# Query products in two cuts, x partly normalised by GpSimd, key normalisation shared in more ways, and a new order

## The chip, the cores and the metric

The kernel runs on one core of a Trainium2 chip. The core has five engines that run their own queues of instructions and wait for one another through semaphores: TensorE (PE in the profile; its weight loads are PEld), VectorE (DVE), ScalarE (ACT), GpSimd (POOL) and SyncE (SP), which here only starts DMA transfers. The metric is the device time of one execution in microseconds (us); lower is better. The time before is the median of three runs.

## The reference

Two blocks follow one another: linear attention with a learned feature map, and a dense layer pair with SiLU. S = 2048 tokens, D = 640, 32 heads of 20, F = 1728, all in bfloat16.

```python
# x: (1, 2048, 640)
xn  = layernorm(x)
q, k, v = split(xn @ wqkv)                      # 32 heads of 20
pq, pk  = q @ w_phi[h], k @ w_phi[h]            # per head, 20 x 20
phi_q = concat(softmax(pq), softmax(-pq))       # 40 features a head
phi_k = concat(softmax(pk), softmax(-pk))
kv  = sum_s phi_k[s, f] * v[s, d];  z = sum_s phi_k[s, f]
o   = (phi_q @ kv) / (phi_q @ z + 1e-6)
h   = x + concat_heads(o) @ wo
out = h + silu(layernorm(h) @ w1) @ w2
```

## The kernel before

The 2048 tokens lie as 16 tiles of 128. Every step on a tile is a small function op_xx, and one long string, ORDER (line 25), lists all steps as words such as `kp.4@0`: step kp for tile 4, with its result in PSUM bank 0. The words are issued in that order with a manual schedule, so ORDER fixes the queue of every engine; an instruction waits for its data, and for the buffer or bank that it writes, and holds up what stands behind it in its own queue. PSUM has eight banks. Most products take two (@4 is 4 and 5), dp takes four, and bank 7 collects the keys' sums (KV).

The stages, with the words used in the text:

- Weights of the keys: `wm` are matmuls on constants that warm TensorE up; `wt` transposes a block of the key weights on TensorE and `wc` copies it out; `fk`/`fc` fold w_phi into it. `gk`/`gc` do the same for the query weights, whose transposes come by DMA (`lq`), into the memory that held the key weights.
- x: `st` the statistics (VectorE), `rs` the reciprocal deviation (mostly GpSimd), `xn` the normalised tile, by VectorE (`.v`) or ScalarE (`.a`); `xt`/`xc` transpose it on TensorE and copy it (tiles 0 to 3), `xd` transposes it by DMA (the other twelve).
- Keys and values: `kp`, `vp` the products (ten matmuls of 320 columns, L368), `vc` the copy of V, `ke` the two exponentials (ScalarE), `kr` the sums of the softmax and their reciprocals (VectorE, L401, L404), `kn` the multiplication by them (L411 on GpSimd, L415 on VectorE), `cc` the sum over tokens into bank 7 (L424, 32 matmuls a tile). `kn.t.p` is all on GpSimd; with `.b` half of the 1,280 elements are VectorE's.
- `kc`, `km`: the sums leave bank 7 (ScalarE), are transposed and masked (VectorE; `mc`, `mt` make the mask).
- Queries: `qp.g.i` the product for four tiles, g, and two (i = 0, 1) or one (i = 2) of five blocks of features, ten or five matmuls of 512 columns (L455), `qe` its two exponentials.
- `dp` numerators and denominators of a tile (40 small matmuls, L490, four banks); `dw` joins the two halves on VectorE (L508 to L514) and with that frees the banks; `dr` a reciprocal (L519), `do` the two halves of the output (GpSimd `.p` or VectorE `.v`, L525), `td` a DMA transpose, `op` the product with wo (L552), `oa` adds it to x (VectorE, L561).
- Second block: `sq`, `sr`, `hn` the layer norm, `hd` a DMA transpose, `up` the product with w1 (L631) for a group of two or four tiles, `ua` SiLU (ScalarE, L653), `yp`, `yh` the product with w2 (L677, L690), `yo` adds and stores; tile 13 ends in two parts (`yz`).

Of the kernel before, what the change touches and what calls it, by code (L numbers as in the profile page):

```python
# [743 lines left out]
```

## Time and profile before

| what | value |
| --- | --- |
| median of 3 runs | 238.31 us (237.97 to 238.56) |
| profiled execution | 238.42 us, span 236.6 us |
| busy: PE, DVE, ACT, POOL | 229.5, 133.0, 117.6, 94.7 us |
| key stage (24.0 to 64.4 us): PE, DVE, ACT, POOL | 40.29, 37.79, 33.88, 38.40 of 40.4 us |
| dp stage (66.9 to 107.4 us): PE, DVE, ACT, POOL | 38.36, 32.25, 25.78, 18.93 of 40.5 us |
| granted TensorE clock | 1.00 throughout |

A row of the profile names the line, engine and operation, what is written and read, and the shape. In groups, the numbers behind the bar are busy time in us, mean ns of one, and idle time of the engine before them with what ended it; in the timeline, a row begins with its start and its length in us, rows of the same kind are merged (x20 is twenty instructions), and a bracket tells how long the engine stood idle before and who ended that. Matmul records are pipelined, so a lone one lasts longer than its slot, and one or two in a hundred are missing.

### The profile page before, as it was taken

Reading aid. Unit: us, or ns where it says so; the run is one execution under the profiler, and the core shown is the slowest. Engines: PE = TensorE matmul, PEld = TensorE weight load, DVE = VectorE, ACT = ScalarE, POOL = GpSimd, SP = SyncE. Lnnn points to the kernel's source line nnn. Section 1 sums busy time; section 2 is a strip of 40 time slices with the busy share of each in tenths; the row PEclk is TensorE's granted clock in tenths of the full one; section 3 lists DMA queues with packets and bytes.
Section 4 is the critical chain, followed back from the end, with each engine's and each line's share of the span. In section 5 each row is a group of like instructions: output and inputs, shape, how many; then the busy total and the mean of one; then the engine's idle time right before and its main releaser. Section 6 shows DMA issues by size and latency. Waiting matters only on the chain.

```text
span 236.6 us, 6282 instructions
## 1 busy us (share of the span) xinstructions
PE 229.5 (97%) x2651; PEld 148.4 (63%) x2672; DVE 133.0 (56%) x250; ACT 117.6 (50%) x175; POOL 94.7 (40%) x187
## 2 busy tenths in 40 slices
PE   8999999999998999999999999999999999999995
PEld 4767777776554455876655576754446667578762
DVE  3999998997858989769785467240002101121122
ACT  3979999878676575755142473412463140303200
POOL 7437889999923543845023057600000310000000
PEclk9999999999999999999999999999999999999999
DMA  7988766990001199464347400654000000040011
GB/s 208 340 310 119 83 146 130 160 261 7 3 3 30 28 194 187 53 150 83 93 38 79 77 0 19 128 127 95 0 3 0 0 28 30 14 124 30 11 47 55
DMA packets 44844, 20.67 MB, mean 87 GB/s; under 512 B 34448, under 2 KB 44304, under 8 KB 44816
## 3 DMA queue, kind: packets, MB, share of 16 engines
q1 hardware_dynamic: 43728, 19.88, 39.1%
q10 hardware_dynamic: 1088, 0.39, 0.7%
q8 instruction: 21, 0.34, 0.7%
q14 instruction: 7, 0.06, 0.1%
HBM read 9.61 MB, written 2.62 MB: 52 GB/s over the span
## 4 chain that ended last, share of the span: by engine, by line
PE 86%; DMA 5%; DVE 4%; ACT 2%; issue 1%; SPq 1%; DVEq 0%; ACTq 0%
PE mm L677 24%; PE mm L631 22%; PE mm L368 17%; PE mm L552 8%; PE mm L455 7%; DMA wv<-in_A_wqkv_dram 3%; PE mm L490 2%; PE mm L424 2%; DMA X<-in_A_x_dram 1%; PE mm L641 1%; PE mm L690 1%; DVE u L511 1%; DVE u L514 1%; ACT EqT L465 1%; ACT sq L569 1%
## 5 line engine op out<-in xcount | busy, mean ns | idle before, releaser
L653 ACT ACTIVATE shT<-mm 128x1024 bf16<-128x1024 f32 (+2 forms) x29 | 27.5, 962 | 64.4 <-PE mm L631 55.8
L631 PE MATMUL mm<-HnT,w 128*128 128x512 bf16 (+1 forms) x315 | 58.1, 335 | 0.9 <-ACT shT L653 0.2
L677 PE MATMUL mm<-w,shT 128*128 128x320 bf16 (+2 forms) x415 | 58.3, 299 | 0.1
L677 PEld LDWEIGHTS <-shT 128*128 128x128 bf16 x416 | 39.7, 98 | 17.6 <-issue 1.3
L631 PEld LDWEIGHTS <-w 128*128 128x128 bf16 x325 | 31.4, 98 | 23.3 <-issue 0.4
L368 PEld LDWEIGHTS <-XnT 128*128 128x128 bf16 x320 | 30.8, 98 | 12.7 <-issue 0.8
L411 POOL TENSOR_TENSOR Ek<-Ek,Sk 128x1280 bf16<-128x1280 bf16 (+1 forms) x16 | 35.7, 2266 | 1.0 <-DVE Sk L404 1.0
L698 DVE TENSOR_TENSOR ob<-mm,X 128x640 bf16<-128x640 f32 x15 | 12.2, 823 | 40.6 <-PE mm L690 19.3
L561 DVE SCALAR_TENSOR_TENSOR X<-mm,X 128x640 bf16<-128x640 f32 x16 | 13.1, 819 | 29.1 <-PE mm L552 29.1
L525 POOL TENSOR_TENSOR o<-u,rd 128x320 bf16<-128x320 f32 x21 | 15.9, 778 | 23.5 <-DVE rd L519 15.9
L465 ACT ACTIVATE EqT<-mm 128x1024 bf16<-128x1024 f32 (+1 forms) x24 | 19.6, 884 | 10.2 <-PE mm L455 10.1
L368 PE MATMUL mm<-wv,XnT 128*128 128x320 bf16 x160 | 24.0, 299 | 0.4 <-DMA wv<-in_A_wqkv_dram 0.3
L401 DVE TENSOR_REDUCE Sk<-Ek 128x64 f32<-128x1280 bf16 x16 | 23.2, 1448 | 1.8 <-ACT Ek L393 1.8
L368 PE MATMUL mm<-Wfk,XnT 128*128 128x320 bf16 x160 | 23.9, 299 | 0.0
L552 PE MATMUL mm<-wo,ot 128*128 128x320 bf16 x160 | 23.6, 299 | 0.2 <-ACT EqT L465 0.2
L455 PE MATMUL mm<-XnT,Wfq 128*128 128x512 bf16 x90 | 21.9, 379 | 1.2 <-issue 0.9
L393 ACT ACTIVATE Ek<-mm 128x640 bf16<-128x640 f32 x32 | 20.5, 717 | 3.7 <-PE mm L368 3.6
L574 POOL TENSOR_SCALAR hm<-hst 128x1 f32<-128x1 f32 x16 | 3.2, 198 | 47.2 <-DVE X L561 47.2
L552 PEld LDWEIGHTS <-ot 128*128 128x128 bf16 x160 | 15.3, 98 | 7.2 <-issue 0.7
L569 ACT ACTIVATE sq<-X 128x640 bf16<-128x640 bf16 x16 | 11.7, 734 | 11.1 <-DVE X L561 9.4
L271 DVE BATCH_NORM_STATS2 stats<-X 128x6 f32<-128x320 bf16 x32 | 13.7, 470 | 4.2 <-DMA X<-in_A_x_dram 4.1
L455 PEld LDWEIGHTS <-Wfq 128*128 128x128 bf16 x100 | 9.1, 98 | 9.7
(77 smaller groups left out, 217.4 us busy)
## 6 DMA issues: line engine op xcount, KB each, us to landing
out_dram<-ob SPq DMA_DIRECT2D x15, 160.0 KB, 1.8
w<-in_B_w_dram SPq DMA_DIRECT2D x6, 360.0 KB, 3.9
X<-in_A_x_dram SPq DMA_DIRECT2D x3, 640.0 KB, 9.4
w<-in_B_w_dram SPq DMA_DIRECT2D x5, 320.0 KB, 3.4
wk<-in_A_wqkv_dram SPq DMA_DIRECT2D x4, 160.0 KB, 3.7
wv<-in_A_wqkv_dram SPq DMA_DIRECT2D x1, 480.0 KB, 7.9
wo<-in_A_wo_dram SPq DMA_DIRECT2D x1, 480.0 KB, 11.9
w<-in_B_w_dram SPq DMA_DIRECT2D x1, 480.0 KB, 5.1
```

What stands on the lines that cost most here:

```text
L368: nc.tensor.matmul(ps[:, half, 0:320], tok(XnT[t // GT], t)[:, c, :], W[:, c, half * 320 : (half + 1) * 320], start=(c == 0), stop=(c == C ...
L393: nc.scalar.activation(Ek[:, s, :].rearrange("p (a n) -> p a n", a=2), tl["kp", t][:, :, 0:320], AF.Exp, scale=1.0 - 2.0 * s,)
L401: nc.vector.tensor_reduce(Sk[:], tl["ek", t][:].rearrange("p s (h f) -> p (s h) f", f=DH), axis=AX.X, op=ALU.add,)
L411: nc.gpsimd.tensor_tensor(Ek3[:, 0:n], Ek3[:, 0:n], Sk[:, 0:n].unsqueeze(2).to_broadcast([P, n, DH]), op=ALU.mult,)
L455: nc.tensor.matmul(ps[:, k, :], Wfq[:, c, r * P : (r + 1) * P], XnT[g][:, c, :], start=(c == 0), stop=(c == C - 1),)
L465: nc.scalar.activation(E[:, s, rs[0] : rs[-1] + 1, :], tl["qp", g, i][:, 0 : len(rs), :], AF.Exp, scale=1.0 - 2.0 * s,)
L525: (nc.vector if eng == "v" else nc.gpsimd).tensor_tensor(tl["o", t][:, a * 320 : (a + 1) * 320].rearrange("p (h f) -> p h f", f=DH), tl["u ...
L552: nc.tensor.matmul(ps[:, half, 0:320], tl["ot", t][:, c, :], wo[:, c, half * 320 : (half + 1) * 320], start=(c == 0), stop=(c == C - 1),)
L569: nc.scalar.activation(sq[:], X[:, t, :], AF.Square, accum_out=tl["hst", t][:, 1:2])
L631: nc.tensor.matmul(ps[:, i * W : (i + 1) * W], w1[:, c, fc * P : (fc + 1) * P], HnT[g][:, c, 0:W], start=(c == 0), stop=(c == C - 1), skip ...
L653: nc.scalar.activation(sh[:, a:b], tl["up", g, k][:, 0 : b - a], AF.Silu)
L677: nc.tensor.matmul(ps, shT[g][:, fc * W + i * P : fc * W + (i + 1) * P], w2[:, fc, a:b], start=first and fc == 0, stop=last and fc == FC - ...
```

## The change

All 16 tiles, products, shapes and roundings stay. Four things are changed.

- `xn` may run on GpSimd (`.p`), with VectorE's instruction. Ten tiles do: 0, 1, 4, 5, 8, 10, 11, 12, 13, 14. ScalarE has four left of nine, VectorE two of seven.
- `kn` gets two more ways of sharing: `.d` gives GpSimd 16 of the 64 head softmaxes, `.v` none; `.q` (48) is used now. In the new order GpSimd has all of tiles 2, 4, 5, 6, 9, 10, 11, 12, 14; 48 of 64 of 0, 7, 15; 32 of 3; 16 of 1 and 8; none of 13.
- The query product is issued in cuts: `qp` the first two matmuls of the first block, `qs` its other three, `qr` and `qt` the same for the second block.
- ORDER is written anew for all engines, with other banks, and with five warm-up matmuls of 256 columns behind `wt.0` where there were one of 256 and one of 128. Some copies change engine: `fc.2`, `vc.13` to VectorE, `wc.4`, `wc.2` to ScalarE, `wc.1` to VectorE; seven layer norms `hn` and nine output halves `do` change sides.

The functions:

```diff
     def op_xn(t, eng):
...
-        if eng == "v":
-            nc.vector.tensor_scalar(
+        if eng != "a":
+            (nc.vector if eng == "v" else nc.gpsimd).tensor_scalar(
                 out=xn[:], in0=X[:, t, :], scalar1=mv[:, 0:1], scalar2=rstd[:, 0:1],
...
     def op_kn(t, split="p"):
...
-        n = {"p": 2 * H, "q": 48, "b": H}[split]
-        nc.gpsimd.tensor_tensor(
-            Ek3[:, 0:n], Ek3[:, 0:n], Sk[:, 0:n].unsqueeze(2).to_broadcast([P, n, DH]), op=ALU.mult,
-        )
+        n = {"p": 2 * H, "q": 48, "b": H, "d": 16, "v": 0}[split]
+        if n > 0:
+            nc.gpsimd.tensor_tensor(
+                Ek3[:, 0:n], Ek3[:, 0:n], Sk[:, 0:n].unsqueeze(2).to_broadcast([P, n, DH]), op=ALU.mult,
+            )
...
     QR = [(0, 1), (2, 3), (4,)]
 
+    def qcut(g, i, k, cs):
+        r = QR[i][k]
+        for c in cs:
+            nc.tensor.matmul(
+                tl["qp", g, i][:, k, :], Wfq[:, c, r * P : (r + 1) * P], XnT[g][:, c, :],
+                start=(c == 0), stop=(c == C - 1),
+            )
+
     def op_qp(g, i):
-        ps = mm2() if len(QR[i]) == 2 else mm1().unsqueeze(1)
...
+        tl["qp", g, i] = mm2() if len(QR[i]) == 2 else mm1().unsqueeze(1)
+        qcut(g, i, 0, range(2))
+
+    def op_qs(g, i):
+        qcut(g, i, 0, range(2, C))
+
+    def op_qr(g, i):
+        qcut(g, i, 1, range(2))
+
+    def op_qt(g, i):
+        qcut(g, i, 1, range(2, C))
```

ORDER before, up to the first key products, and from the end of the key stage through the dp stage:

```
mk mo lx.0.1.a st.0 rs.0.1 lk.0.1.s lp.a ph.v wm.512@7 wm.512@7 wm.512@7 wm.512@7 wm.512@7 wm.512@7 wm.512@7
wm.512@7 wm.512@7 wm.256@7 wt.0@0 lx.1.2.s lk.4.5.a lk.1.2.s wm.256@2 wm.128@2 wt.1@1 st.1 lk.2.3.s lk.3.4.s
ta wt.2@2 wc.2.v wc.0.a fk.0@4 wt.3@3 wc.1.a fc.0.a fk.1@6 fc.1.a fk.2@0 fc.2.a wc.3.v wt.4@2 rs.1.2 xn.0.v
wc.4.v fk.3@4 fc.3.a lx.2.4.s xn.1.v lx.8.12.s xt.0@3 fk.4@6 fc.4.a lv.0.3.s xc.0.v st.2 rs.2.3 xt.1@2
xc.1.a lv.3.5.s st.8 st.9 rs.8.10 kp.0@0 ke.0 xn.2.v lx.4.8.s st.3 rs.3.4 st.11 lx.12.16.s kp.1@4 vp.1@6
...
vc.7.a ke.7 qp.0.1@2 kr.15 qe.0.1 cc.6 cc.10 kr.7 cc.13 cc.8 kn.15.p qp.0.0@0 qe.0.0 vp.14@4 vc.14.a
qp.0.2@6 l2.2.4.s kn.7.b cc.15 cc.7 qe.0.2 mc.1 mt cc.14 kc km.0 l1.5.s km.1 qp.3.0@2 dp.0@4 qe.3.0 qp.2.0@0
qe.2.0 close dw.0.p dr.0 do.0.0.p do.0.1.p dp.1@2 qp.1.0@6 dw.1.p dr.1 do.1.0.p dp.3@0 dw.3.p dr.3 qe.1.0
do.3.0.p qp.1.1@4 qe.1.1 td.0 do.3.1.p dp.2@0 dw.2.p dr.2 qp.1.2@6 qe.1.2 do.1.1.p td.1 op.0@4 oa.0 l2.6.8.s
dp.4@0 dw.4.p dr.4 do.2.0.p do.2.1.p td.2 sq.0 qp.2.1@6 qe.2.1 qp.2.2@4 qe.2.2 l1.4.s l1.1.s sr.0 hn.0.v
dp.6@0 dw.6.p qp.3.2@5 do.4.1.p qe.3.2 op.1@6 oa.1 sq.1 dp.5@0 dw.5.p op.2@4 do.4.0.p qp.3.1@6 qe.3.1 sr.1
td.4 hn.1.v oa.2 dp.9@0 dw.9.p sq.2 sr.2 hn.2.a td.3 op.3@4 oa.3 sq.3 op.4@6 l1.2.s hd.0 hd.1 dr.5 do.5.1.p
do.5.0.p hd.2 oa.4 sq.4 dr.6 dp.7@0 dw.7.p up.0.2@4 ua.0.2 do.6.1.p up.0.0@6 ua.0.0 dp.8@0 dw.8.p dr.8
...
```

ORDER after, the same stretches and the key stage between them:

```
mo lx.0.1.a lk.0.1.s lp.a wm.512@7 wm.512@7 wm.512@7 wm.512@7 wm.512@7 wm.512@7 wm.512@7 wm.512@7 wm.512@7
wm.256@7 wt.0@0 st.0 lx.1.2.s lk.4.5.a ta mk rs.0.1 wm.256@2 wm.256@2 wm.256@2 wm.256@2 wm.256@2 wt.4@1
lk.1.2.s wt.1@2 ph.v lk.2.3.s st.1 xn.0.p wc.1.v rs.1.2 xn.1.p wt.2@3 wc.0.a fk.0@4 lk.3.4.s wt.3@6 wc.3.v
wc.4.a xt.0@7 xc.0.v wc.2.a fc.0.a fk.1@0 fc.1.a fk.2@2 fc.2.v lx.2.4.s st.2 fk.3@4 fc.3.a rs.2.3 mc.0
fk.4@6 fc.4.a lx.8.12.s st.3 xn.2.v xt.1@0 xc.1.a st.8 lv.0.3.s kp.0@2 ke.0 rs.3.4 kp.1@4 xt.2@1 xc.2.a ke.1
lv.3.5.s vp.0@6 vc.0.a xn.3.a vp.2@2 vc.2.a st.9 lx.4.8.s rs.8.10 xn.8.p xn.9.a st.10 kp.2@0 st.11 rs.10.12
xt.3@4 vp.1@6 xc.3.a st.5 lx.12.16.s vc.1.a kp.3@2 ke.3 ke.2 xn.10.p vp.3@4 vc.3.a xn.11.p lq.1.s gk.1@6
gc.1.a xd.8 vp.8@2 xd.9 kp.9@0 ke.9 vc.8.a xd.10 kp.10@4 ke.10 xd.11 kp.11@6 lq.3.s st.4 rs.4.6 st.13 st.12
rs.12.14 kp.8@0 ke.8 xn.5.p l1.5.s st.15 st.14 rs.14.16 l1.0.s vp.10@2 vc.10.a xn.15.a vp.9@4 xn.12.p xd.12
kr.0 gk.3@0 gc.3.a vp.11@2 vc.11.a vc.9.a xn.4.p xd.4 vp.4@0 vc.4.a kr.3 kn.3.b kp.4@2 ke.11 xn.14.p lh.s
kp.12@4 kn.0.q lq.4.s cc.0 kr.9 xd.15 kn.9.p cc.9 kr.2 xd.5 kn.2.p cc.2 kr.10 cc.3 ke.12 st.6 xn.13.p ke.4
kp.5@0 ke.5 vp.12@4 vc.12.a vp.15@2 vc.15.a vp.5@0 vc.5.a xd.14 st.7 rs.6.8 xn.6.a gk.4@4 gc.4.a l2.10.13.s
kr.1 kp.14@2 ke.14 lo.2.5.s kn.1.d kn.10.p l2.0.2.s xn.7.v xd.7 vp.7@0 kp.7@4 vc.7.a kr.12 kn.12.p kr.11
lq.2.s vp.14@2 vc.14.a gk.2@0 xd.13 gc.2.a kr.5 cc.10 kr.8 lq.0.s kn.11.p kr.14 kn.5.p cc.12 ke.7 kn.8.d
cc.1 cc.5 kr.4 kr.7 cc.11 kn.14.p kn.4.p kn.7.q lo.0.2.s gk.0@2 gc.0.a kp.15@0 ke.15 xd.6 kr.15 kp.6@4 ke.6
kp.13@2 vp.6@0 vc.6.a qp.0.0@4 qs.0.0 qr.0.0 ke.13 qt.0.0 kr.6 qe.0.0 qp.0.1@0 l2.2.4.s qs.0.1 l1.3.s cc.4
kn.15.q l1.4.s cc.15 cc.7 kn.6.p cc.14 qr.0.1 qt.0.1 vp.13@2 qe.0.1 kr.13 kn.13.v qp.0.2@6 vc.13.v mc.1 cc.6
mt cc.8 cc.13 kc qs.0.2 qe.0.2 km.0 qp.3.0@4 qs.3.0 qr.3.0 km.1 dp.0@0 close dw.0.p dr.0 qt.3.0 qp.2.0@6
qs.2.0 qe.3.0 do.0.0.p qr.2.0 qt.2.0 qe.2.0 dp.1@0 qp.1.0@4 qs.1.0 l2.6.8.s do.0.1.p td.0 dw.1.p dr.1 qr.1.0
do.1.0.p l2.4.6.s do.1.1.p qt.1.0 qe.1.0 qp.1.1@6 dp.3@0 dw.3.p dr.3 do.3.1.p qs.1.1 qr.1.1 qt.1.1 qe.1.1
qp.3.2@4 qp.1.2@5 do.3.0.p dp.2@0 dw.2.p dr.2 do.2.0.p do.2.1.p qs.1.2 qe.1.2 td.1 qs.3.2 qe.3.2 l1.2.s
op.0@6 oa.0 dp.4@0 dw.4.p qp.2.2@5 td.3 sq.0 td.2 sr.0 qs.2.2 qe.2.2 hn.0.a op.1@6 oa.1 sq.1 sr.1 hd.0
qp.2.1@4 l1.1.s dp.6@0 dw.6.p hn.1.v qs.2.1 qr.2.1 qt.2.1 qe.2.1 op.3@6 oa.3 sq.3 sr.3 dp.5@0 dw.5.p hd.1
op.2@4 oa.2 dr.5 do.5.0.p l2.8.10.s qp.3.1@6 qs.3.1 qr.3.1 sq.2 dp.9@0 dw.9.p qt.3.1 up.0.2@4 dr.4 dr.9
do.5.1.p td.5 do.9.1.p qe.3.1 do.4.0.p do.4.1.v dp.7@0 dw.7.p up.0.0@6 ua.0.2 dr.7 do.7.0.v td.4 ua.0.0
up.0.3@4 ua.0.3 dp.8@0 dw.8.p sr.2 dr.6 do.6.0.p op.5@6 oa.5 do.7.1.p do.6.1.v td.6 up.0.1@4 ua.0.1 hn.2.a
hd.2 dp.12@0 dw.12.p sq.5 sr.5 td.7 hn.3.v hd.3 op.4@6 oa.4 sq.4 yp.1.0@4 sr.4 hn.5.v hd.5 hn.4.a dp.10@0
dr.12 do.12.1.p yp.1.1 dw.10.p do.9.0.v td.9 yp.0.1@6 yh.0.0 yo.1 dp.11@0 dw.11.p dr.8 do.8.0.v hd.4 dr.11
...
```

61 lines of the change are left out of this document (14 added, 47 removed).

## The prediction

> **What bounds the kernel now.** I read the page first, then TensorE's timeline, then the other engines' timelines and groups beside the places where TensorE waits.
>
> ```profile
> PE 229.5 (97%) x2651; PEld 148.4 (63%) x2672; DVE 133.0 (56%) x250; ACT 117.6 (50%) x175; POOL 94.7 (40%) x187
> ```
>
> TensorE (PE) is busy 97% of the span, so a new order can win only what TensorE stands still, and loses whatever it is made to wait. Neither version changes its arithmetic beyond the warm-up matmuls, so I look for its waits. There are two places. The first is the start (columns: start us, duration us, engine, line, operation, count):
>
> ```profile
> 9.65 2.89 PE L368 MATMUL mm<-Wfk,XnT 128*128 128x320 bf16 x20
> 12.60 0.57 PE L368 MATMUL mm<-wv,XnT 128*128 128x320 bf16 x3
> 13.49 1.11 PE L368 MATMUL mm<-wv,XnT 128*128 128x320 bf16 x7 [0.32 <-DMA wv<-in_A_wqkv_dram]
> ```
>
> A 320-column matmul costs 0.136 us back to back ((2.89 less the 0.17 by which a lone one outlasts its slot) / 20). Twenty from 9.65 end their slots at 12.37, but vp.1 starts at 12.60; its first three end theirs at 13.01, but the fourth starts at 13.49, when wv is there. That is 0.23 + 0.48 = 0.71 us lost. The second place is the stage of the denominators and numerators (dp, L490):
>
> ```profile
> 69.57 2.10 PE L455 MATMUL mm<-XnT,Wfq 128*128 128x512 bf16 x9 [0.16 <-issue]
> 71.61 0.19 PE L490 MATMUL mm<-KVBD,EqT 32*128 32x44 bf16 x2
> 72.09 0.45 PE L490 MATMUL mm<-KVBD,EqT 32*128 32x44 bf16 x38 [0.29 <-DVE u L514]
> 72.70 2.11 PE L455 MATMUL mm<-XnT,Wfq 128*128 128x512 bf16 x9 [0.16 <-issue]
> 74.74 0.19 PE L490 MATMUL mm<-KVBD,EqT 32*128 32x44 bf16 x2
> 75.11 0.45 PE L490 MATMUL mm<-KVBD,EqT 32*128 32x44 bf16 x38 [0.17 <-DVE u L514]
> 75.71 2.11 PE L455 MATMUL mm<-XnT,Wfq 128*128 128x512 bf16 x9 [0.16 <-issue]
> 78.13 0.46 PE L490 MATMUL mm<-KVBD,EqT 32*128 32x44 bf16 x40 [0.31 <-DVE u L514]
> 78.52 1.25 PE L455 MATMUL mm<-XnT,Wfq 128*128 128x512 bf16 x4
> 79.85 1.52 PE L552 MATMUL mm<-wo,ot 128*128 128x320 bf16 x10
> ...
> 92.42 1.53 PE L552 MATMUL mm<-wo,ot 128*128 128x320 bf16 x10
> 94.12 1.52 PE L552 MATMUL mm<-wo,ot 128*128 128x320 bf16 x10 [0.16 <-ACT EqT L465]
> ...
> 100.44 0.47 PE L490 MATMUL mm<-KVBD,EqT 32*128 32x44 bf16 x40
> 101.14 2.34 PE L631 MATMUL mm<-HnT,w 128*128 128x256 bf16 x20 [0.23 <-ACT shT L653]
> ```
>
> A query product has ten matmuls; the row counts nine and the "issue" gap of 0.16 is the record that is missing, so ten take 2.17 us and one 0.217. A dp is a burst of 0.40 us (78.13 to 78.52). dp.1 could go on at 71.62 and does at 72.09; dp.3 at 74.75, and does at 75.11; dp.2 could start at 77.72 (ten products from 75.55) and does at 78.13. The five products from 78.52 fill 1.08 us, and op.0 starts at 79.85; the ten matmuls from 92.42 fill 1.36, and the next start at 94.12; the dp at 100.44 fills 0.40, and the next matmul starts at 101.14. Together 0.47 + 0.36 + 0.41 + 0.25 + 0.34 + 0.30 = 2.1 us. The reason stands in VectorE's rows for one tile:
>
> ```profile
> 72.69 0.36 DVE L508 RECIPROCAL w<-mm 128x32 f32<-128x32 f32 x1 [0.27 <-PE mm L490]
> 73.08 0.19 DVE L509 TENSOR_TENSOR w<-w,mm 128x32 f32<-128x32 f32 x1
> 73.31 0.86 DVE L511 TENSOR_TENSOR u<-mm,w 128x672 f32<-128x672 f32 x1
> 74.20 0.85 DVE L514 TENSOR_TENSOR u<-u,mm 128x672 f32<-128x672 f32 x1
> 75.09 0.35 DVE L519 RECIPROCAL rd<-u 128x32 f32<-128x32 f32 x1
> ```
>
> dw holds the four banks of a dp from 72.69 to 75.05, 2.36 us. Two dp that share banks must stand 0.40 + 2.36 + about 0.1 for two hand-overs = 2.9 us apart; one query product between them gives 2.57.
>
> **The dp stage, changed.** Every dp but two now sits on banks 0 to 3, and the cut products let other amounts of work stand between: 13, 12, 12 product matmuls after dp.0, dp.1, dp.3 (spacing 3.2, 3.0, 3.0 us), then 6 or 5 or 7 of them and one wo product (1.36 us): 3.1 to 3.5 us. All are over 2.9, so the three waits of dp above go; those behind 78.52, 92.42 and 100.44 stand at places that the new order fills otherwise. What is late next is VectorE's own queue: from oa.0 on it also has to do these between two dw:
>
> ```profile
> L561 DVE SCALAR_TENSOR_TENSOR X<-mm,X 128x640 bf16<-128x640 f32 x16 | 13.1, 819 | 29.1 <-PE mm L552 29.1
> ...
> L295 DVE TENSOR_SCALAR xn<-X,MV,RS 128x640 bf16<-128x640 bf16 x7 | 3.6, 518 | 0.0
> ```
>
> With oa (0.82), dr (0.35) and sometimes a layer norm or an output half (about 0.5, like L295), a tile costs it 3.5 to 4.0 us against 3.3 of TensorE. Walking both queues from dp.0, it falls behind at dw.5: op.2 then waits some 0.25 us for its banks, dp.9 0.25, dp.7 0.3, after which two feed-forward products (over 3 us) let it catch up. I put 0.85 us of waiting there (the three and a little), with 0 and 2.1 (as now) as ends. The stage gains 2.1 - 0.85 = 1.25. The cuts add no matmul; the order of accumulation is the same.
>
> **The start, changed.** x of tiles 0 and 1 is normalised by GpSimd, behind its own chain of the deviation:
>
> ```profile
> 6.59 0.26 POOL L281 TENSOR_SCALAR RS<-MV,RS 128x1 f32<-128x1 f32 x1
> 8.02 0.67 POOL L279 TENSOR_TENSOR RS<-RS,nhalf 128x1 f32<-128x1 f32 x1 [1.17 <-DVE RS L276]
> 8.79 0.45 POOL L281 TENSOR_SCALAR RS<-MV,RS 128x1 f32<-128x1 f32 x1
> ```
>
> No row shows xn (640 elements) on GpSimd. The nearest are its one-input selection of 288 elements and its two-input multiplication of 640 (three rows of it, the last one undisturbed):
>
> ```profile
> L212 POOL TENSOR_SCALAR_AFFINE_SELECT maskR<-maskR 128x288 bf16<-128x288 bf16 x1 | 0.5, 501 | 0.1
> ```
>
> ```profile
> 41.47 2.36 POOL L411 TENSOR_TENSOR Ek<-Ek,Sk 128x1280 bf16<-128x1280 bf16 x1 [0.57 <-DVE Sk L404]
> 43.79 1.85 POOL L411 TENSOR_TENSOR Ek<-Ek,Sk 128x640 bf16<-128x640 bf16 x1
> 45.60 1.26 POOL L411 TENSOR_TENSOR Ek<-Ek,Sk 128x640 bf16<-128x640 bf16 x1
> ```
>
> By proportion the selection gives 1.11 us, with its fixed part counted more than twice; the multiplication, 1.26, is the upper end, and half of it, 0.63, the lower (one input in place of two). I take 1.0, near the selection, which also reads one input. The deviation of tile 0 is there at 6.85 as now, xn.0 at 7.85; that of tile 1 takes 1.1 more (0.67 + 0.45), so xn.1 is there at about 10.0, xt.1 ends at 10.4 and kp.0 starts there, not at 9.65: +0.75. The longer warm-up lies in front of this wait and costs nothing more; without it it would cost some 0.4 (896 columns more at 0.136 for 320). But vp.0 now comes after kp.0, kp.1 and xt.2, at 10.4 + 2.72 + 0.28 = 13.4, when wv is just landing (13.49), so the 0.71 goes. One later small wait (kp.3 behind ScalarE's copy of XnT, which now stands behind two normalisations) adds 0.1. Sum of the start: +0.2, from -0.1 (xn at 0.63) to +0.5 (1.26). The loads in front are the same; wo's two move from behind the last x to the middle, and the first weight transpose takes their place, with 2 us to spare by the same walk. The transposes of x stand in SP's queue in the order of their tiles; each now waits for GpSimd where it waited for VectorE or ScalarE, and by the walk the first one (tile 8) lands some 1.5 us before vp.8 needs it.
>
> **The key normalisation.** GpSimd gains ten xn (10 us) and loses 2,880 of the 18,560 elements it multiplied (5 us by the 1,280-element row below). Five of the ten lie before 24 us, where it is half idle. VectorE is the tight one:
>
> ```profile
> 14.70:64.40 49.70, 49.59 (x762) 35.70 (x762) 46.78 (x71) 41.87 (x67) 43.93 (x43) 1.00 0.63 122
> ```
>
> Its 46.78 of 49.70 us leave 2.9. (Columns: window, length, busy PE, PEld, DVE, ACT, POOL.) What a piece of the key normalisation costs it depends on GpSimd. Two of its three pieces now, beside GpSimd's rows above:
>
> ```profile
> 43.18 1.33 DVE L415 TENSOR_TENSOR Ek<-Ek,Sk 128x640 bf16<-128x640 bf16 x1
> ...
> 62.66 1.67 DVE L415 TENSOR_TENSOR Ek<-Ek,Sk 128x640 bf16<-128x640 bf16 x1
> ```
>
> GpSimd's multiplication ends at 43.83 and VectorE's, begun at 43.18, ends 0.68 later at 44.51; GpSimd's next is 0.59 longer than its like at 45.60. They take turns: VectorE's piece waits for GpSimd's instruction under way, then runs 0.68 us per 640 elements. [...] That speaks against sharing in more pieces, since each piece adds a wait. Charged at the 1.33 of the row, the 2,880 added elements would cost 6.0 us; by turns they cost 3.1 and the waits.
>
> VectorE's sum: 4,800 elements against 1,920, +3.1; waits for the port by my walk 3.7 us, against 0.65 and 0.99 in the two rows, so some 2.4 at three pieces, +1.3; five xn fewer at 0.52, -2.6; two copies from PSUM more (like oa, 0.82) and one smaller less, +1.1; its own later start +0.7. That is +3.6 on an end at 64.33 (62.66 + 1.67), less the idle time that goes, since the keys come earlier than VectorE needs them (2.4 of the 2.9): 65.5. TensorE reaches the last cc here:
>
> ```profile
> 65.82 0.93 PE L424 MATMUL mm<-Ek,Vp 128*21 128x40 bf16 x96
> ```
>
> It ends at 66.75 now; the change has three query matmuls fewer in front (0.65) and the start's +0.2, and the last cc starts 0.3 before its end: 66.0. VectorE's margin of 0.5 is smaller than what the waits may be off by, so I charge 0.2, from 0 to 2.4 (one whole GpSimd multiplication). Behind it in VectorE's queue are the copy of V for tile 13 and the mask transpose, and behind the last cc the chain kc, km, dp.0; ten query matmuls (2.17 us) cover that chain as now.
>
> **The rest.** From 107 us on I followed bank by bank who must be done before each feed-forward group starts. The smallest margins are about 0.7 to 1 us (the transpose of tile 4 before up.1.6, of tile 8 before up.2.6), so I put 0 there, and 0.5 if one is missed. Output halves and layer norms change sides between GpSimd, ScalarE and VectorE where all three stand idle more than half of the time. The tail is the same: two parts of tile 13.
>
> **Sum.** The profiled execution took 238.42 us, 0.11 above the median of the three runs, 238.31; what lies around its span is taken to stay. 238.42 + 0.2 (start) + 0.2 (keys) - 1.25 (dp stage) = 237.57, and 0.11 less against the median: 237.46, given as 237.4.
>
> **Rivals.** (1) Slower: turns at the port. When kr.6 ends, GpSimd's kn.6 (2.36) and VectorE's last part of kn.15 (0.35) become ready together; if GpSimd goes first, cc.15, which has next to no margin, waits 2.3 us. One lost turn of this kind decides it: 237.4 + 2.3 = 239.7. For it: seven pieces in place of three, and a VectorE without idle time. Against: VectorE needs no signal from another engine there, and in both rows above it came second only because GpSimd was already running. (2) The dp stage's waits go entirely and xn takes 0.63: 237.4 - 0.85 - 0.3 = 236.3. For it: between the dp VectorE's work averages less than TensorE's, tiles without oa included. Against: from dp.4 on it is the longer of the two. (3) The change doesn't do what it says: VectorE's queue sets the dp stage whatever stands between, the waits only move, and 237.4 + 1.25 = 238.7; or xn costs 1.26 or more and pushes back the first keys (238 or so). [...]
>
> **How the numbers follow.** Chances: forecast 0.42, rival (1) 0.25, (2) 0.17, (3) 0.16. The likeliest one's own range is 236.7 to 238.2; with the ends of the others, 235.9 to 239.8. About 0.3% (0.7 us) can be told from no change. Faster by more than that (under 237.6): all of (2) and over three quarters of the forecast, 0.51. Slower (over 239.0): (1) and a little of (3), 0.28. Within: 0.21.
>
> **What would show it.** Right: no VectorE wait in front of dp.1, dp.3, dp.2; kp.0 at about 10.4 and no wait for wv; xn on GpSimd near 1.0 us. Wrong: a wait in front of the cc group of tiles 4, 15, 7, 14 or of the last one; VectorE's kn pieces over 2 us; dp of tiles 5, 9, 7 waiting more than 0.5 each.

## The result and the profile after

| kernel | median | ratio to before |
| --- | --- | --- |
| before | 238.3 us (237.97 to 238.56) | 1 |
| changed | 250.83 us (250.63 to 250.94) | 1.0526 [1.0511, 1.0542] |

I had forecast 237.4 us, 235.9 to 239.8. The change is 12.5 us slower. The page of the changed kernel, first the busy times, then the chain that ended last:

```profile
PE 231.9 (93%) x2675; PEld 148.3 (60%) x2675; DVE 134.1 (54%) x250; ACT 110.8 (44%) x166; POOL 116.5 (47%) x196
...
PE 68%; POOL 15%; DVE 11%; issue 3%; DMA 1%; ACT 1%; DVEq 0%; POOLq 0%
```

TensorE falls from 97% to 93% of a longer span, GpSimd (POOL) goes from 94.7 to 116.5 us, and it holds 15% of the chain. One group is new, of 25.0 us; against it the multiplications of the keys fall from 35.7 to 30.2 us, and the rest changes little (busy time, mean ns):

```profile
L297 POOL TENSOR_SCALAR xn<-X,MV,RS 128x640 bf16<-128x640 bf16 x10 | 25.0, 2503 | 0.0
```

One xn takes GpSimd 2.50 us, where I had put 1.0 with 1.26 as the upper end. TensorE's waits name the places (total, times, longest; L427 are the cc products):

```profile
PE mm L370 <- DMA XnT<-xn: 6.6, 2, 5.8
PE mm L308 <- POOL xn L297: 3.4, 2, 1.8
PE mm L427 <- POOL Ek L414: 2.8, 3, 1.4
```

TensorE's timeline at the start and at tile 4 (L308 is xt, L370 kp and vp):

```profile
9.33 0.45 PE L308 MATMUL mm<-ident,xn 128*128 128x128 bf16 x5 [1.78 <-POOL xn L297]
9.62 1.43 PE L337 MATMUL mm<-phb,wTk 128*128 128x140 bf16 x24
12.70 0.45 PE L308 MATMUL mm<-ident,xn 128*128 128x128 bf16 x5 [1.66 <-POOL xn L297]
12.99 2.88 PE L370 MATMUL mm<-Wfk,XnT 128*128 128x320 bf16 x20
...
35.55 1.52 PE L370 MATMUL mm<-wv,XnT 128*128 128x320 bf16 x10
42.83 2.83 PE L370 MATMUL mm<-wv,XnT 128*128 128x320 bf16 x10 [5.77 <-DMA XnT<-xn]
45.48 2.76 PE L370 MATMUL mm<-Wfk,XnT 128*128 128x320 bf16 x19
```

kp.0 starts at 12.99 and not at 9.65. The product at 42.83 is vp.4: it waits 5.77 us for the transposed tile 4, and then its ten matmuls need 2.65 us and not 1.36. The granted clock is the share of its full speed at which TensorE was let run. The windows (length, then busy PE, PEld, DVE, ACT, POOL, and the granted clock before the DMA share) show that it changed:

```profile
42.80:45.40 2.60, 2.57 (x10) 1.49 (x11) 0.00 (x0) 0.00 (x0) 2.60 (x2) 0.50 0.55 129
45.50:48.00 2.50, 2.50 (x20) 1.81 (x19) 0.00 (x0) 1.90 (x3) 2.50 (x3) 1.00 0.65 122
```

After the wait TensorE is granted half its clock, 0.50, for those 2.6 us: the 5.77 us cost another 1.3. What tile 4 waited for stands in GpSimd's timeline:

```profile
31.03 2.51 POOL L297 TENSOR_SCALAR xn<-X,MV,RS 128x640 bf16<-128x640 bf16 x1
...
35.19 5.00 POOL L297 TENSOR_SCALAR xn<-X,MV,RS 128x640 bf16<-128x640 bf16 x2
40.15 1.28 POOL L414 TENSOR_TENSOR Ek<-Ek,Sk 128x640 bf16<-128x640 bf16 x1
```

xn.4 is the second of the two from 35.19. It ends at 40.19, its transpose lands 2.6 us later, and vp.4 starts at 42.83. GpSimd has no gap between these rows; it is simply late, and the key multiplications behind it are late too (the cc products' 2.8 us). dp.0 starts at 82.30 against 68.94. From there on the first three dp go as forecast (L457 the query products, L504 dp):

```profile
82.30 0.46 PE L504 MATMUL mm<-KVBD,EqT 32*128 32x44 bf16 x40
82.70 2.98 PE L457 MATMUL mm<-XnT,Wfq 128*128 128x512 bf16 x13
85.61 0.47 PE L504 MATMUL mm<-KVBD,EqT 32*128 32x44 bf16 x40
86.01 2.76 PE L457 MATMUL mm<-XnT,Wfq 128*128 128x512 bf16 x12
88.71 0.47 PE L504 MATMUL mm<-KVBD,EqT 32*128 32x44 bf16 x40
89.11 2.76 PE L457 MATMUL mm<-XnT,Wfq 128*128 128x512 bf16 x12
91.80 0.47 PE L504 MATMUL mm<-KVBD,EqT 32*128 32x44 bf16 x40
```

The last three dp are dp.1, dp.3 and dp.2. No bracket stands in these rows: they wait for nothing.

### The profile page after: what moved, and what is told of

Its sections match the earlier page's. It is cut to its first block, busy times and chain, and to the rows that moved or that the text cites. A ratio compares the mean times of both kernels' runs of the same rounds, so it can differ in the third digit from the quotient of the medians.

```text
span 249.0 us, 6305 instructions
## 1 busy us (share of the span) xinstructions
PE 231.9 (93%) x2675; PEld 148.3 (60%) x2675; DVE 134.1 (54%) x250; ACT 110.8 (44%) x166; POOL 116.5 (47%) x196
## 4 chain that ended last, share of the span: by engine, by line
PE 68%; POOL 15%; DVE 11%; issue 3%; DMA 1%; ACT 1%; DVEq 0%; POOLq 0%
PE mm L645 23%; PE mm L691 23%; PE mm L566 8%; POOL xn L297 8%; PE mm L457 8%; DVE Sk L403 5%; POOL Ek L414 3%; PE mm L504 2%; POOL RS L281 2%; DVE stats L273 2%; DVE Sk L406 1%; DVE Ek L418 1%; DMA X<-in_A_x_dram 1%; PE mm L655 1%; PE mm L704 1%
## 5 line engine op out<-in xcount | busy, mean ns | idle before, releaser
L691 PE MATMUL mm<-w,shT 128*128 128x320 bf16 (+2 forms) x416 | 58.9, 299 | 0.0
L645 PE MATMUL mm<-HnT,w 128*128 128x512 bf16 (+1 forms) x325 | 58.8, 337 | 0.1
L667 ACT ACTIVATE shT<-mm 128x1024 bf16<-128x1024 f32 (+2 forms) x29 | 27.0, 962 | 42.4 <-PE mm L645 41.7
L370 PEld LDWEIGHTS <-XnT 128*128 128x128 bf16 x320 | 31.3, 99 | 19.6 <-DMA XnT<-xn 7.2
L414 POOL TENSOR_TENSOR Ek<-Ek,Sk 128x1280 bf16<-128x1280 bf16 (+3 forms) x15 | 30.2, 2039 | 0.6 <-DVE Sk L406 0.5
L370 PE MATMUL mm<-wv,XnT 128*128 128x320 bf16 x160 | 25.0, 310 | 5.8 <-DMA XnT<-xn 5.8
L539 POOL TENSOR_TENSOR o<-u,rd 128x320 bf16<-128x320 f32 x24 | 17.4, 742 | 27.7 <-DVE rd L533 27.7
L297 POOL TENSOR_SCALAR xn<-X,MV,RS 128x640 bf16<-128x640 bf16 x10 | 25.0, 2503 | 0.0
L370 PE MATMUL mm<-Wfk,XnT 128*128 128x320 bf16 x160 | 23.4, 299 | 0.8 <-DMA XnT<-xn 0.8
L457 PE MATMUL mm<-XnT,Wfq 128*128 128x512 bf16 x100 | 23.8, 380 | 0.0
L171 ACT CAST Vp<-mm 128x640 bf16<-128x640 f32 x15 | 10.4, 702 | 12.7 <-PE mm L370 12.6
```

The costliest lines, as they stand in the source:

```text
L297: (nc.vector if eng == "v" else nc.gpsimd).tensor_scalar(out=xn[:], in0=X[:, t, :], scalar1=mv[:, 0:1], scalar2=rstd[:, 0:1], op0=ALU.subt ...
L370: nc.tensor.matmul(ps[:, half, 0:320], tok(XnT[t // GT], t)[:, c, :], W[:, c, half * 320 : (half + 1) * 320], start=(c == 0), stop=(c == C ...
L414: nc.gpsimd.tensor_tensor(Ek3[:, 0:n], Ek3[:, 0:n], Sk[:, 0:n].unsqueeze(2).to_broadcast([P, n, DH]), op=ALU.mult,)
L457: nc.tensor.matmul(tl["qp", g, i][:, k, :], Wfq[:, c, r * P : (r + 1) * P], XnT[g][:, c, :], start=(c == 0), stop=(c == C - 1),)
L539: (nc.vector if eng == "v" else nc.gpsimd).tensor_tensor(tl["o", t][:, a * 320 : (a + 1) * 320].rearrange("p (h f) -> p h f", f=DH), tl["u ...
L645: nc.tensor.matmul(ps[:, i * W : (i + 1) * W], w1[:, c, fc * P : (fc + 1) * P], HnT[g][:, c, 0:W], start=(c == 0), stop=(c == C - 1), skip ...
```

## The experiments

Theory: the whole loss is the 2.50 us of an xn on GpSimd (called dear below, in contrast to a cheap form found on the way). Rival: the new order, or the turns of VectorE and GpSimd in the shared key normalisation, lose a good part. The table has where TensorE stood in each run's timeline, in us. Each ratio is to a before measured beside the run, whose median was 238.04 to 238.34; between runs measured at different times, compare the ratios.

| kernel | kp.0 | dp.0 | median | ratio to before, 95% |
| --- | --- | --- | --- | --- |
| before | 9.65 | 68.94 | 238.30 | 1 |
| changed | 12.99 | 82.30 | 250.83 | 1.0526 [1.0511, 1.0542] |
| e1_xn_back | 10.72 | 77.50 | 246.57 | 1.0366 [1.0340, 1.0392] |
| g1_xn_back_early | 10.52 | 71.87 | 240.06 | 1.0079 [1.0062, 1.0096] |
| e2_xn_alone | 14.46 | 89.30 | 259.10 | 1.0878 [1.0856, 1.0899] |
| f2_mult_add_alone | 11.21 | 76.80 | 246.38 | 1.0335 [1.0307, 1.0363] |
| e5_sharing_alone | 9.97 | 75.05 | 242.26 | 1.0191 [1.0156, 1.0226] |
| f1_mult_add | 10.05 | 69.18 | 237.65 | 0.9980 [0.9971, 0.9989] |
| h1_cc_later | 10.24 | 69.26 | 237.64 | 0.9982 [0.9972, 0.9991] |
| d1_two_dear | 13.16 | 70.85 | 239.36 | 1.0066 [1.0040, 1.0092] |
| e3_cuts_alone | 9.90 | 68.70 | 236.84 | 0.9940 [0.9922, 0.9959] |
| h2_cuts_alone_filled | 9.93 | 68.11 | 236.49 | 0.9936 [0.9922, 0.9950] |

**The ten xn put back** (e1_xn_back). Ten words of the changed order:

```diff
-xn.0.p xn.1.p xn.4.p xn.5.p xn.8.p xn.10.p xn.11.p xn.12.p xn.13.p xn.14.p
+xn.0.v xn.1.v xn.4.a xn.5.v xn.8.a xn.10.a xn.11.v xn.12.a xn.13.a xn.14.v
```

> The changed kernel with the ten xn taken off GpSimd and put where the kernel before has them (0, 1, 5, 11 and 14 on VectorE, 4, 8, 10, 12 and 13 on ScalarE); the cut query products, the key-normalisation sharing and the new order stay. Theory A: the loss is the 2.50 us that one xn takes on GpSimd, ten times, and nothing else. Then kp.0 starts near 10 us again (12.99 in the changed kernel), the waits of the transposes for xn (1.94 and 1.81 us) and of vp.4 for its transfer (5.93 us) are gone, dp.0 starts near 69 to 70 us (82.30), and the time is 236.5 to 239.0 us, the lower end if the 1.24 us of the dp stage stay whole. Rival B: a good part of the loss is the new order and the turns of VectorE and GpSimd in the shared key normalisation. Then the waits of the cc products for Ek (1.52, 1.06 and 0.52 us) stay and the time is 241 to 246 us.

It took 246.57 us: a miss for theory A, and just over rival B's number, though by another way than B's, as no cc product waited for Ek. The wait for tile 4 was still there, 4.96 us and the 1.28 of half clock behind it (0.50 granted from 41.2 to 43.8 us), now through ScalarE (timeline; L170 are copies of V):

```profile
36.43 1.29 ACT L170 CAST Vp<-mm 128x640 bf16<-128x640 f32 x2
37.60 0.93 ACT L301 ACTIVATE xn<-X,RS 128x640 bf16<-128x640 bf16 x1
```

xn.4 stood behind copies that wait for TensorE, and TensorE's next product waited for xn.4. So the run had undone the price, but had put ten instructions into queues whose places were written for another engine. What it could not tell was whether the order is bad or only not made for this.

**The ten xn alone** (e2_xn_alone). The order of before, with the same ten words set to `.p`.

> The order of the kernel before with one thing changed: the same ten xn on GpSimd. No cut of the query products takes effect (the parts stand together) and the key normalisation is shared as before. Theory A: ten xn of 2.50 us on GpSimd, 25 us of which the stage up to dp.0 has to find room; time 248 to 254 us, the upper end because this order was not made for a late tile 4. Rival B: 239.5 to 244 us, since the order of before is kept and the new one is what loses.

259.10 us, over the range of theory A: here vp.5 (tile 5) waits longest, 9.48 us, and runs at a granted clock of 0.50 (49.1 to 51.6 us):

```profile
L296 POOL TENSOR_SCALAR xn<-X,MV,RS 128x640 bf16<-128x640 bf16 x10 | 25.0, 2509 | 0.0
```

```profile
49.07 2.85 PE L369 MATMUL mm<-wv,XnT 128*128 128x320 bf16 x10 [9.48 <-DMA XnT<-xn]
```

The xn alone lose more (20.8 us) than the whole change does (12.5).

**The cuts, without the rest** (e3_cuts_alone). The order of before up to the last cc, from kc on the changed one (two of its load words stand where this order still needs them):

```diff
-cc.14 kc km.0 l1.5.s km.1 qp.3.0@2 dp.0@4 qe.3.0 qp.2.0@0 ...
+cc.14 kc qs.0.2 qe.0.2 km.0 l1.5.s qp.3.0@4 qs.3.0 qr.3.0 km.1 dp.0@0 close dw.0.p ...
```

> The order of the kernel before up to the last cc product, then from kc on the order of the changed kernel with its query products in steps of two and three matmuls; no xn on GpSimd, key normalisation shared as before. My step of the prediction: the stage from qp.3.0 to yp.1.0 loses 1.64 us of TensorE in place of 2.88, so the time is 236.8 to 237.5 us, 0.9 to 1.5 under the kernel before. Rival: the waits only move to the products behind (up and yp have no slack to lend) and the time is 238.0 to 238.6 us.

236.84 us, 1.50 under the 238.34 of the before beside it, where the step had 1.25. That is less than 1%, but the interval, 0.9922 to 0.9959, lies clear of 1. The step stands, with one limit: from kc on the run has the new order, banks and changes of engine too, so it does not show what the cut by itself is worth.

**What GpSimd charges** (e4_prices). Ten instructions on dead data behind hn.15:

```diff
+        for n in (320, 640, 1280):
+            g.tensor_scalar(out=b[:, 0:n], in0=a[:, 0:n], scalar1=m, scalar2=r, op0=ALU.subtract, op1=ALU.mult)
+        g.tensor_scalar(out=b[:, 0:640], in0=a[:, 0:640], scalar1=r, scalar2=m, op0=ALU.mult, op1=ALU.add)
...
```

> The kernel before with ten more GpSimd instructions behind hn.15 on data that is dead by then; nothing reads what they write. In order: tensor_scalar subtract and mult with two per-partition scalars at 320, 640 and 1280 elements; mult and add with two per-partition scalars, with two immediates, with one of each, all at 640; mult alone with one per-partition scalar; a copy; a product of two tensors; a product with a broadcast column. What it prices is the one figure that the prediction took wrongly (1.0 us, at most 1.26, for what took 2.50). Theory A: the price is that of the elements with two per-partition scalars, about 3.8 ns an element: 1.25 to 1.35, 2.5 and 4.9 us at the three sizes, and 1.0 to 1.3 us for the forms with immediates. Rival C: 2.5 us is a fixed setting up of per-partition scalars: then 2.2, 2.5 and 3.0 us. Rival D: every tensor_scalar of two operations on bf16 is as dear, immediates too. The time itself stays within 1 us of the kernel before, as nothing waits for GpSimd there.

The groups, kept apart by shape (L715 subtract and mult; L716 mult and add, two per-partition scalars; L717 the same with immediates; L718 mult and mult, one of each; L719 mult alone; L720 a copy; L721 a product of two tensors; the tenth, a product with a broadcast column, took 1.25 us as well):

```profile
L715 POOL TENSOR_SCALAR Wfq<-Wfq,MV,RS 128x320 bf16<-128x320 bf16 x1 | 1.5, 1453 | 0.0
L715 POOL TENSOR_SCALAR Wfq<-Wfq,MV,RS 128x640 bf16<-128x640 bf16 x1 | 2.5, 2502 | 0.1
L715 POOL TENSOR_SCALAR Wfq<-Wfq,MV,RS 128x1280 bf16<-128x1280 bf16 x1 | 4.7, 4680 | 0.1
L716 POOL TENSOR_SCALAR Wfq<-Wfq,RS,MV 128x640 bf16<-128x640 bf16 x1 | 0.9, 877 | 0.1
L717 POOL TENSOR_SCALAR Wfq<-Wfq 128x640 bf16<-128x640 bf16 x1 | 0.7, 727 | 0.1
L718 POOL TENSOR_SCALAR Wfq<-Wfq,RS 128x640 bf16<-128x640 bf16 x1 | 0.8, 799 | 0.1
L719 POOL TENSOR_SCALAR Wfq<-Wfq,RS 128x640 bf16<-128x640 bf16 x1 | 1.9, 1892 | 0.1
L720 POOL COPY Wfq<-Wfq 128x640 bf16<-128x640 bf16 x1 | 0.7, 717 | 0.1
L721 POOL TENSOR_TENSOR Wfq<-Wfq 128x640 bf16<-128x640 bf16 x1 | 1.3, 1254 | 0.1
```

None of the three theories. Theory A has the three sizes nearly right, but not the reason: the per-partition scalars cost 0.15 us (877 against 727). What is dear is the pair of operations: 3.4 ns an element for subtract and mult ((4680 - 1453) / 960), 0.88 us in all for mult and add. The kernel itself took 245.14 us in its one run, and my "nothing waits for GpSimd there" was wrong: hn.14 needs a scalar that GpSimd computes behind the ten (ScalarE's waits; TensorE in turn waits 4.5 us for the transpose of hn):

```profile
ACT hn L598 <- POOL hm L595: 16.0, 6, 8.1
```

**Which operations are dear** (p2_prices). Eight more, this time behind hn.14, where they delay nobody (237.98 us in one run).

> The kernel before with eight more GpSimd tensor_scalar behind hn.14 on dead data; nothing reads what they write. In order, at 640 elements with two per-partition scalars: add and mult, mult and mult, mult and subtract, subtract and add; then subtract and mult with immediates, mult alone with an immediate; then mult and add with two per-partition scalars at 320 and 1280. The first price run had 2.50 us for subtract and mult, 0.88 for mult and add, both with two per-partition scalars. Theory A: the first operation being subtract (or add) is the dear thing, so add-mult, subtract-add and the immediate subtract-mult take 2.3 to 2.5 us and mult-mult and mult-subtract 0.8 to 0.9. Rival B: mult followed by add is the one cheap pair, all others 1.9 to 2.5 us. Rival C: subtract in either place is dear, add-mult cheap.

L715's four in their order, add and mult, mult and mult, mult and subtract, subtract and add, each from a timeline of its own window; then subtract and mult with immediates (L718) and mult alone with one (L719):

```profile
195.20 0.98 POOL L715 TENSOR_SCALAR Wfq<-Wfq,RS,MV 128x640 bf16<-128x640 bf16 x1
...
196.28 0.88 POOL L715 TENSOR_SCALAR Wfq<-Wfq,RS,MV 128x640 bf16<-128x640 bf16 x1
...
197.26 2.52 POOL L715 TENSOR_SCALAR Wfq<-Wfq,RS,MV 128x640 bf16<-128x640 bf16 x1
...
199.88 2.52 POOL L715 TENSOR_SCALAR Wfq<-Wfq,RS,MV 128x640 bf16<-128x640 bf16 x1
...
202.49 2.35 POOL L718 TENSOR_SCALAR Wfq<-Wfq 128x640 bf16<-128x640 bf16 x1
204.93 1.82 POOL L719 TENSOR_SCALAR Wfq<-Wfq 128x640 bf16<-128x640 bf16 x1
```

Rival C: a pair with a subtract in either place costs 2.35 to 2.52 us, a pair made of add and mult 0.73 to 0.98. A lone mult is dear as well, 1.82 to 1.89. Why GpSimd does so, no run here shows.

**The decisive run: one instruction** (f1_mult_add). The same x normalised, written so that GpSimd meets no subtract; rstd[:, 1:2] is -mean times rstd, which the kernel computes already. The order is the changed one, word for word:

```diff
-        if eng != "a":
-            (nc.vector if eng == "v" else nc.gpsimd).tensor_scalar(
+        if eng == "p":
+            nc.gpsimd.tensor_scalar(
+                out=xn[:], in0=X[:, t, :], scalar1=rstd[:, 0:1], scalar2=rstd[:, 1:2],
+                op0=ALU.mult, op1=ALU.add,
+            )
+        elif eng != "a":
+            nc.vector.tensor_scalar(
...
```

> The changed kernel, its order word for word, with one line changed: xn on GpSimd is x times rstd plus (-mean times rstd), a mult and an add with two per-partition scalars, instead of (x minus mean) times rstd, a subtract and a mult. The price run had 0.88 us for the one at 640 elements and 2.50 us for the other, so 16 us of GpSimd go away and nothing else moves. Theory A: the order is sound and was made for an xn of about this price; the 250.83 us come from the 2.50 us alone. Then xn.4 ends before 33 us (40.2 in the changed kernel), vp.4 waits for no transfer (5.93 us and 1.28 us of half clock behind it), the cc products wait under 1 us for Ek (3.3), the start term is near my forecast of 10.4 us for kp.0 (12.99), and the time is 236.5 to 239.0 us, so in the forecast range. Rival B, from the run with the ten xn put back (246.57 us): the order holds tile 4 up whatever xn costs, and the time is 243 to 247 us.

237.65 us, 13.2 less than the changed kernel. GpSimd's group, and its row with xn.12 and xn.4:

```profile
L297 POOL TENSOR_SCALAR xn<-X,RS 128x640 bf16<-128x640 bf16 x10 | 10.5, 1052 | 0.4
```

```profile
26.79 2.65 POOL L297 TENSOR_SCALAR xn<-X,RS 128x640 bf16<-128x640 bf16 x2
```

xn.4 ends at 29.44 and not at 40.19. TensorE meets kp.0 at 10.05 and runs through tile 4:

```profile
10.05 2.96 PE L375 MATMUL mm<-Wfk,XnT 128*128 128x320 bf16 x20
...
31.70 2.88 PE L375 MATMUL mm<-wv,XnT 128*128 128x320 bf16 x20
34.42 1.79 PE L375 MATMUL mm<-Wfk,XnT 128*128 128x320 bf16 x12
```

Only the form of ten instructions differs, and vp.4 waits no more: the price of xn is the cause of the loss, and the order is sound for an xn of the forecast price. It wins little even so, 0.48 us against the before beside it.

**The same instruction in the order of before** (f2_mult_add_alone).

> The order of the kernel before with the ten xn on GpSimd in the mult and add form (0.88 us each), no cut in effect, key normalisation as before; its counterpart with the subtract form took 259.1 us. Theory A: the price makes most of the 20.8 us; 8.8 us of GpSimd in place of 25. Then 239 to 243 us, still over the kernel before since this order has xn.4 and xn.12 behind kn.1 and others on GpSimd. Rival B: GpSimd's place in the order is what counts and not the price: 248 us and more.

246.38 us: 12.7 less than with subtract, so the price is the larger part here too, but 8.2 over the before beside it and above theory A's range. In an order that did not provide for it even a cheap xn comes late (vp.5 waits 3.09 us for its transfer, and loses 1.28 more at a granted clock of 0.50).

**The sharing alone** (e5_sharing_alone). Nine kn words of before's order: tiles 2 and 5 all on GpSimd, 3 by halves, 1 and 8 mostly and 13 all on VectorE, 0, 7 and 15 as 48 and 16.

> The kernel before with the shared key normalisation of the changed kernel alone: nine kn words take its forms (tiles 3, 2, 1, 8, 13, 5, 0, 7 and 15), at their old places; xn as before, query products whole. My step: the pieces that VectorE takes cost it 0.39 to 0.68 us each in turns with GpSimd and give GpSimd the same back; between 0 and 2 us worse at places that were not made for it. Theory A (sharing is harmless): 237.8 to 240.3 us. Rival B: the turns cost TensorE directly, over 242 us, and so explain a good part of the 8.2 us that stayed when the ten xn were put back.

242.26 us, a miss for theory A's range, and by the number alone just in rival B's. The loss begins on VectorE: kr.4 (L402, L405) stands behind VectorE's half of tile 3 (L417), and kn.4 on GpSimd, the last row, waits for kr.4:

```profile
40.21 1.89 DVE L417 TENSOR_TENSOR Ek<-Ek,Sk 128x640 bf16<-128x640 bf16 x1
42.03 1.47 DVE L402 TENSOR_REDUCE Sk<-Ek 128x64 f32<-128x1280 bf16 x1
43.53 0.55 DVE L405 RECIPROCAL Sk<-Sk 128x64 f32<-128x64 f32 x1
```

```profile
44.23 2.35 POOL L413 TENSOR_TENSOR Ek<-Ek,Sk 128x1280 bf16<-128x1280 bf16 x1 [2.81 <-ACT Vp L170]
```

The bracket names ScalarE's copy of V, which ends at almost the same time, but kn.4 reads only Ek and Sk. In the kernel before kr.4 ended at 41.33 and kn.4 began at 41.47. Of VectorE's 1.89 us, 1.21 lie in front of 41.42, where GpSimd's multiplication under way ends, and 0.68 behind it. Behind kn.4 GpSimd now has tiles 2 and 5 whole, so kn.5 ends at 51.20 and kn.12 at 53.52, and the cc products wait for both:

```profile
51.26 1.26 PE L426 MATMUL mm<-Ek,Vp 128*21 128x40 bf16 x128 [1.52 <-POOL Ek L413]
53.58 0.45 PE L426 MATMUL mm<-Ek,Vp 128*21 128x40 bf16 x32 [1.06 <-POOL Ek L413]
53.96 2.85 PE L369 MATMUL mm<-Wfk,XnT 128*128 128x320 bf16 x10
56.60 2.87 PE L369 MATMUL mm<-wv,XnT 128*128 128x320 bf16 x10
```

The two products behind those waits take 2.65 us each, at a granted clock of 0.50: 2.6 us for two short waits close together. These rows are of the slowest of the six executions (244.91 us, mean granted clock 0.986). In four of the six the mean clock was 0.998 or more and the time 241.76 to 242.58 us, so the median holds little of those 2.6 us, and some 4 us are left to the late tiles. So the added pieces do cost time in an order not made for them, though not as rival B had it, on TensorE directly, but through VectorE's queue and then GpSimd's; how much of it is turns and how much the other shares no run separates. The decisive run has the same shares in the new order and is, with all its parts, 0.48 us under its before.

**xn put back, two of them early** (g1_xn_back_early).

```diff
-rs.4.6 st.13 st.12 rs.12.14 kp.8@0 ... xn.12.a xd.12 ... vc.9.a xn.4.a xd.4
+rs.4.6 xn.4.a st.13 st.12 rs.12.14 xn.12.a kp.8@0 ... xd.12 ... vc.9.a xd.4
```

> The changed kernel with the ten xn put back on VectorE and ScalarE (which took 246.57 us), and two of them earlier in ScalarE's queue: xn.4 right behind rs.4.6 and xn.12 right behind rs.12.14. In that run vp.4 waited 4.96 us for its transfer and then ran 1.28 us longer at half the granted clock, because xn.4 started only at 37.6, behind three copies of V that wait for TensorE. Theory A: this place in ScalarE's queue made most of the 8.2 us that stayed; xn.4 then ends before 33 us, vp.4 no longer waits, and the time is 239.0 to 241.5 us. Rival B: VectorE and ScalarE are too full for the ten xn in this order, the wait only moves to another tile, and the time stays at 244 us or more.

240.06 us: two words moved win 6.5 us, about the 4.96 and 1.28 that vp.4 had lost, and vp.4 waits no more. What the first run had shown was, in the main, the place of xn.4 in ScalarE's queue.

**Two dear, eight cheap** (d1_two_dear). xn.0 and xn.1 with subtract and mult, the others as in the decisive run.

> The changed kernel with two dear xn in place of ten: tiles 0 and 1 keep subtract and mult (2.50 us), the eight later ones take mult and add (0.87). Between all dear (250.83 us) and none (237.65) it gives the share of the start. Theory A: waits on TensorE add up; kp.0 starts at 12.9 again, 2.9 us after that of the run with none (10.05), nothing behind is lost or won back, and the time is 240.2 to 241.0 us. Rival B: a later start gives GpSimd and VectorE time to run ahead and the waits for Ek behind it (0.8 us) go: 239.4 to 240.1 us. Rival C: the dear pair delays the later xn on GpSimd too, over 241.5 us.

239.36 us, at the lower edge of rival B. kp.0 is 3.1 us later than with none dear, dp.0 only 1.7: the later start lets the multiplications run ahead, and no wait of cc for Ek is left in the list. So the two dear xn at the start cost 1.7 us by themselves. The other 11.5 of the 13.2 come only when the eight behind are dear too; eight dear ones alone were not run.

**Two small moves** (h1_cc_later, h2_cuts_alone_filled). In the decisive run's order cc.1 behind cc.11, cc.5 behind gk.0, `qr.0.1 qt.0.1` in front of cc.15; and in the order of the run with the cuts `qs.0.2` in front of the last cc.

> The changed kernel with the mult and add form (237.65 us) and three small moves on TensorE: cc.1 behind cc.11, cc.5 behind gk.0, and the last two parts of qp.0.1 in front of cc.15, so that work that is ready stands before the two waits for GpSimd's Ek (0.31 and 0.53 us). Theory: the 0.7 to 0.9 us of those waits go, 236.7 to 237.1 us. Rival: the chain behind the last cc ends as late as before, since GpSimd's kn.6 sets it, and the time is 237.4 to 237.9 us.

> The order of before with the cut query products from kc on (236.84 us), and the second part of qp.0.2 moved from behind kc to in front of the last cc, which there waits about 0.3 us for ScalarE's copy of vp.14. Theory: the part fills the wait, 0.2 to 0.4 us less, 236.4 to 236.7 us. Rival: the copy sets dp.0 through kc and km, whatever stands in front, and the time is the same, 236.7 to 237.0 us.

The first did nothing (237.64, the rival's number): the two waits went, and one stood in their place, not for GpSimd's kn.6 but for the copy of V that VectorE makes last:

```profile
66.69 0.37 PE L431 MATMUL mm<-Ek,Vp 128*21 128x40 bf16 x32 [0.70 <-DVE Vp L168]
```

The second took 236.49 us, 0.35 less, the number of its theory, and the last cc no longer waits. But the before beside it was 0.30 lower as well: the ratios, 0.9936 and 0.9940, do not differ by more than their intervals, and a gain is not shown. These two are the fastest runs, 0.6% under before. The decisive run's interval, 0.9971 to 0.9989, lies clear above theirs: xn on GpSimd and the shared key normalisation, with the order that goes with them, lose about 1 us even at the cheap price.

## Why the prediction was wrong

- **The step that failed** is the price of xn: "I take 1.0, near the selection", with 1.26 as "the upper end". It measured 2.50. The two rows I had were of other operations, and I treated them as if GpSimd's time went by the number of elements and of inputs. By that reasoning mult and add fits (0.87) and subtract and mult does not. A pair of operations not seen in the trace had no upper end there, and I gave it one 26% above my value.
- **The start**, forecast +0.2 with kp.0 at 10.4, had 12.99. With mult and add it was 10.05, and vp.0 met wv without a wait, as forecast. The term's upper end was also worked out wrongly: xn.0 and xn.1 follow one another in that chain, so an xn of 1.26 delays kp.0 by 0.52 and not by 0.26, which makes +0.7 and not +0.5.
- **The key stage**, "I charge 0.2, from 0 to 2.4": GpSimd's ten xn were counted as 10 us beside 5 saved; they were 25. That gave vp.4's 7.2 us with its half clock (which the sum did not contain at all), 1.0 at kp.11 and some 3 at the cc products. With mult and add, the cc products wait 0.31, 0.53 and 0.2 us.
- **The dp stage**, -1.25: nearly right, at some -1.4. From the start of qp.3.0 to that of the first yp TensorE stood still about 3.0 us before and 1.6 in the changed kernel, by the prediction's slots (the 2.88 of an expectation above leaves out 0.16 in front, where a record is missing). The waits of dp.1, dp.3 and dp.2, which are gone, made up most of that (0.47 + 0.36 + 0.41). What else comes and goes in the stage nearly cancels, as the sum had it, but by luck: of the late waits put in for VectorE's queue only op.2's came, with 0.27, and ScalarE's EqT ended it, not VectorE. The "6 or 5 or 7" product matmuls between the later dp were miscounted too: the rows have six, seven or eight, and five with one wo product would make 2.85 us, not over 2.9.
- **From 107 us on**, 0: right. From the first yp to the end the changed kernel takes 1.23 us more, and has one wo product more there (1.36).
- **The rivals.** The lost turn (1) did not come about: in the decisive run VectorE's part of kn.15 starts at 61.70, ahead of GpSimd's kn.6 at 61.96. No run shows the "port" that the prediction names in this rival and in VectorE's sum; the rows show the turns alone: VectorE's piece of 640 elements ends 0.68 us after GpSimd's multiplication under way, at 44.51 after 43.83 in the kernel before and at 42.10 after 41.42 with the sharing alone. Rival (3) named the mechanism ("xn costs 1.26 or more and pushes back the first keys") and gave it 238, since it followed the lateness to the first keys alone and not down GpSimd's queue to tile 4.

With xn at 1.05 us, near the price that I had assumed, the change takes 237.65 us against my 237.4: 0.48 less than the before beside it, where I had 0.9 less. The parts lie a little further off than their sum: from kc on the order wins 1.50, where I had 1.25, and what stands in front loses about 1 by the two runs, where I had 0.4. One unseen price took the time out of its range.

## What to carry to other kernels

An operation that the trace does not show on an engine has no upper bound from other operations on that engine, least of all ten of them at the head of a queue: take the range to at least twice the nearest row (xn took 2.50 us, where the nearest rows gave 1.11 and 1.26), and follow the lateness through everything queued behind. When a part is undone by changing the engine of a word, the word's place in a queue changes too; keep the place and change the price instead, as the decisive run does. On GpSimd, write a normalisation of this kind (bf16, two per-partition scalars) as mult and add: 0.88 us against 2.50 at 128x640.

## What the hardware showed that I had not expected

- GpSimd's tensor_scalar at 128x640 bf16: 0.73 to 0.98 us for pairs of add and mult, 2.35 to 2.52 with a subtract in either place, 1.82 to 1.89 for a mult alone, against 0.72 for a copy. A mult alone costs more than a mult and an add.
- A wait of TensorE can cost more than its length. The granted clock was 0.50 for 2.6 us after the wait of 5.77 us in the changed kernel and after the one of 3.09 us in the order of before with mult and add, 1.3 us lost each time; and for 5.3 us after two of 1.52 and 1.06 us with 1.26 us of work between, 2.6 us lost. It differs from execution to execution: with the sharing alone four of six had a mean clock of 0.998 or more, with mult and add in the order of before one of four had 1.000 (245.13 us) and three 0.993 (246.18 to 246.67). How long a wait must be for that, no run here shows: after the waits of 1.78 and 1.66 us at the start of the changed kernel the clock was 1.00.
